# Half of one batch's first product as seven block products, sums moved, and a softmax divided later

## The chip, the core and the metric

The kernel runs on one core of a Trainium2 chip. Its engines each work through a queue of their own: TensorE (PE: matmuls; PEld: the loads of their stationary operand), VectorE (DVE), ScalarE (ACT), GpSimd (POOL), and SyncE (SP), which issues transfers. Matmul results land in PSUM, eight banks of 128 partitions x 512 fp32 each; everything else lies in SBUF. The metric is the device time of one execution in microseconds, 204.79 before the change (median of three runs).

## The reference

Per batch and head, tokens `x` (512 x 64) and a state (32 x 64) attend to one another; both results stand as rows of one matrix, which goes through a two-layer network.

```python
scores  = scale * x @ state.T;   a  = softmax(scores);   xread = a @ state     # 512 rows per head
scores2 = scale * state @ x.T;   a2 = softmax(scores2);  sread = a2 @ x        # 32 rows per head
...
x = attn_out.transpose(0, 2, 1, 3).reshape(B * S, H * D)    # B=8, 544 rows each, H*D=512
h = x @ w_in                                                # w_in 512 x 2048
g = np.maximum(0.01 * h, h)
return g @ w_out                                            # w_out 2048 x 512
```

Softmax here divides by the sum of the exponentials plus 1e-9. "Token softmax" is the one over tokens (`a2`).

## The kernel before

**First product.** For the 512 token rows of a batch the kernel does not form `xread`. Since `xread @ w_in = a @ (state @ w_in)`, it computes `M = state @ w_in` per head (`a_m`, psum tile `pm`), a matrix of 256 rows (8 heads x 32 states) and 2048 columns, held in SBUF as two groups of 128 rows, and then `a @ M` with `a` transposed (`aT`, two groups of 128 rows x 512 tokens). `ff1(a, hT, j)` does column block `j` of sixteen: two matmuls of 512 columns into a bank `ph` (line 372), then ACT's leaky relu into `hT[:, j]` (line 377). The tag `ph` has two banks.

**Second product.** From batch 2 on, `hT @ w_out` is done by `Fast` and `Batch`: the matrices are cut into 2 x 2 blocks and seven block products replace eight. Sums of blocks of `hT` (`su`, line 546) and of `w_out` (`tw`, line 523, made once in batch 2 by `weights_sum`) are operands. One *unit* is two matmuls of 256 columns (line 557); a block product has 8 units, numbered `n` in the order 1, 2, 6, 5, 7, 3, 4, and a batch 56. They use two banks (tag `py`, tile `yq`): some block products add onto what is in a bank, and in between the bank is copied out (`save`, line 566, ACT) or added to a saved one (`join`, line 569, DVE, or line 627, POOL).

**Order.** All queues but the transfers' details are written out by hand: `manual_schedule` keeps each engine's instructions in the order in which the program issues them. The loop over batches 2 to 7 has 16 steps `s`. Each step issues `ff1(s)` and then `PACE[s]` units (1 to 4) of the batch before, or, once those are used up, of its own (15 in all). So the units of batch 6 run between the column blocks of batch 7. Between them stand, at fixed steps, the attention of the next batch: scores, both softmaxes (`a_shift`, `a_exp`, `a_probs`; `a_max2`, `a_exp2`, `a_probs2`), `M`. After the loop a tail does the rest of batch 7's units, the first product of the 256 state rows (`FastIn`, also seven block products, whose operands are sums of `w_in`, tile `sw`, made by `w_sum` on DVE, and of `sread`, made by `x_sums`), and their second product.

**Token softmax.** `a_exp2` (ACT) writes the exponentials `e2` and their row sums `r2`. `a_probs2` (step 11 of the batch before, DVE) adds 1e-9, takes the reciprocal and multiplies both halves into `a2` (line 285). `a_a2t` transposes it with a transfer on SP's queue into `a2T` (step 0). At step 10 `a_sread_rows` forms `sread` in a bank of the tag `ph` (`psn`, line 318), and ACT copies it to `sr_n` (line 326). Behind it on PE, `a_m(nxt, 2, "ph")` needs two banks of that tag. Batch 7 differs: `a_sread` (step 8, line 300, tile `psr`) uses `a2T` as the stationary side's partner and writes `sr_t` directly (line 307).

**Places of the moved sums.** `weights_sum(0)` and `(2)` at step 3 of batch 2, `(1)` and `(3)` at step 8. `FastIn.w_sum(0)`, `(1)`, `(2)` at step 4 of batch 7, `(3)` and `x_sums` at step 10. At steps 0 to 3 DVE also makes the second halves of the `su` sums of the batch before, and at step 12 the first halves of its own.

Of the kernel before, what the change touches and what calls it, by code (L numbers as in the profile page):

```python
# [27 lines left out]
def kernel(  # L28
# [111 lines left out]
    st_t = [consts.tile([P, hi - lo, P], BF16, name=f"st_t{lo}") for lo, hi in groups]  # L140
    sr_t = consts.tile([P, B, NK, NS], BF16, name="sr_t")
    sr_n = {}

    stb0 = consts.tile([P, 4, D], BF16, name="stb0")

# [123 lines left out]

    def a_exp2(a, g):  # L270
        if g == 0:
            a.e2 = att.tile([P, 2, S], BF16, name="e2", tag="e2")
            a.r2 = att.tile([P, 2], FP32, name="r2", tag="r2")
        nc.scalar.activation(  # L274
            out=a.e2[:, g], in_=a.sc[:, g, :], func=AF.Exp,
            bias=a.m2s[:, g:g + 1], scale=SCALE, accum_out=a.r2[:, g:g + 1],
        )

    def a_probs2(a):
        nc.vector.tensor_scalar(out=a.r2[:], in0=a.r2[:], scalar1=1e-9, scalar2=None, op0=ALU.add)  # L280
        q2 = att.tile([P, 2], FP32, name="qc", tag="qc")
        nc.vector.reciprocal(q2[:], a.r2[:])
        a.a2 = att.tile([P, 2, S], BF16, name="a2", tag="a2")
        for g in range(2):
            nc.vector.tensor_scalar(
                out=a.a2[:, g, :], in0=a.e2[:, g, :],
                scalar1=q2[:, g:g + 1], scalar2=None, op0=ALU.mult,
            )

    def a_a2t(a):  # L290
        a.a2T = att.tile([P, 2, NT, P], BF16, name="a2T", tag="a2T")
# [19 lines left out]
    def a_sread_rows(some):  # L311

        ps = psum.tile([P, len(some), 2, D], FP32, name="psn", tag="ph")
        for u, a in enumerate(some):
            for g in range(2):
                for i in range(NT):
                    for k in range(NK):
                        nc.tensor.matmul(  # L318
                            ps[NS * k:NS * (k + 1), u, g, :],
                            lhsT=a.a2T[:, g, i, NS * k:NS * (k + 1)], rhs=a.xb[:, i, 2 * k + g, :],  # L320
                            start=(i == 0), stop=(i == NT - 1),
                        )
        c, b0 = divmod(some[0].b, 4)
        if c not in sr_n:
            sr_n[c] = consts.tile([P, 4, P], BF16, name=f"sr_n{c}", tag=("st0f", "stf2")[c])
        nc.scalar.copy(
            sr_n[c][:, b0:b0 + len(some)], ps[:].rearrange("p u g d -> p u (g d)")
        )

    def sread_t(c, n):  # L330
# [59 lines left out]
    class FastIn:  # L390
# [57 lines left out]
        def done(self, r, n, bank):  # L448
            R = self.R
            if n == 1:  # L450
                pool, tag, bufs = ((xpool, "xl", 1), (mpool, "M", 2))[r]
                self.sv[r] = pool.tile([P, 4, R * P], FP32, name=f"sf{r}", tag=tag, bufs=bufs)
            sv = {k: self.sv[r][:, i] for i, k in enumerate((1, 6, 5, 7))}
            flat = bank.rearrange("p q t -> p (q t)")

            def relu(i, c, src):
                nc.scalar.activation(
                    out=self.hT[:, 8 * i + R * r:8 * i + R * (r + 1), P * c:P * (c + 1)],
                    in_=src.rearrange("p (q t) -> p q t", q=R), func=AF.Prelu, alpha=0.01,
                )  # L460

            if n in (1, 6, 7):
                SCA(sv[n], flat)
            elif n == 5:
                VEC(sv[n], flat)
            if n in (2, 3):
                k = {2: 1, 3: 6}[n]
                nc.vector.tensor_tensor(out=sv[k], in0=flat, in1=sv[k], op=ALU.add)
                relu(0, n - 2, sv[k])
            elif n == 7:  # L470
                nc.gpsimd.tensor_tensor(out=sv[5], in0=sv[7], in1=sv[5], op=ALU.add)
            elif n == 4:
                relu(1, 1, sv[5])
                relu(1, 0, flat)

    class Y:
        pass
# [39 lines left out]
    def weights_sum(dst):  # L517
        u, v, op = (
            (B12, B11, ALU.subtract), (B11, tw[2], ALU.subtract),
            (B22, B12, ALU.add), (tw[1], B21, ALU.add),  # L520
        )[dst]
        with nc.allow_low_precision(reason="operands of a product"):
            nc.vector.tensor_tensor(out=tw[dst][:], in0=u[:], in1=v[:], op=op)
# [408 lines left out]
    for b in range(2, B):  # L932
        hT = hpool.tile([P, 16, S], BF16, name="hT", tag="hT")
        a = att_of[b]
        nxt = att_of[b + 1] if b + 1 < B else None
        now = Batch(b, hT)
        std = []
        if b == 2:
            std = [(i, 3) for i in range(2)] + [(i, jq) for i in range(2, NT) for jq in range(4)]

        def fill(s):
            n = (PACE2 if b == 2 else PACE)[s]
            left = min(n, len(before.units)) if before else 0
            if left:
                before.run(left)
            if n > left:
                now.run(n - left)

        for s in range(16):
            if s == 11:  # L950
                fill(s)
            ff1(a, hT, s)
            if s == 0:
                if b + 2 < B:
                    load_x(b + 2, nc.sync)
                    open_xb(b + 2)
                a_a2t(a)
                if before:
                    for n in (0, 1):
                        before.f.sums(n, 4, 8)  # L960
            elif s == 1:
                if nxt is not None:
                    a_scores(nxt)
                m_evict(a, 3, a_m(a, 3, "big"), SCA)
                if b == 2:
                    a_sread_rows([a0])
                if nxt is not None:
                    a_shift(nxt)
                if b + 2 < B:
                    for h in range(0, H, 2):  # L970
                        cast_x(b + 2, h, h + 2, POO)
                if before:
                    before.f.sums(2, 4, 8)
            elif s == 3:
                if before:
                    before.f.sums(3)
                if nxt is not None:
                    a_max2(nxt)
                if b == 2:
                    weights_sum(0)  # L980
                    weights_sum(2)
            elif s == 4:
                if b == 2:
                    state_t(1)
                elif b == 4:
                    sread_t(0, 4)
                elif b == 7:
                    sread_t(1, 3)
            elif s == 8:
                if nxt is None:  # L990
                    a_sread(a)
                if b == 2:
                    weights_sum(1)
                    weights_sum(3)
            elif s == 12:
                for n in range(3):
                    now.f.sums(n, 0, 4)
            if nxt is None:
                if s == 4:
                    fi = FastIn(None)  # L1000
                    for n in range(3):
                        fi.w_sum(n)
                elif s == 10:
                    fi.w_sum(3)
                    fi.x_sums()
            if s == (9 if b == 2 else 7) and b + 2 < B:
                a_open(att_of[b + 2], b + 2)
                a_xt_dma(att_of[b + 2])
            if nxt is not None:
                if s == 5:  # L1010
                    a_exp(nxt)
                elif s in (7, 8):
                    a_exp2(nxt, s - 7)
                    if s == 7:
                        a_probs(nxt)
                elif s == 11:
                    a_probs2(nxt)
                elif s in (12, 13):
                    SCA(nxt.M[:, s - 12, DM:2 * DM], pm1[:, s - 12, :])
            if std:  # L1020
                i, jq = std.pop(0)
                piece(1, h1, i, jq)
            elif s != 11:
                fill(s)
            if s == 10 and nxt is not None:
                a_sread_rows([a1, a2] if b == 2 else [a])
                pm0 = a_m(nxt, 0, "big")
                pm1 = a_m(nxt, 1, "sc")
                pm2 = a_m(nxt, 2, "ph")
                for g, copy in enumerate((VEC, SCA)):  # L1030
                    copy(nxt.M[:, g, 2 * DM:3 * DM], pm2[g][:])
                m_evict(nxt, 0, pm0, SCA)
        before = now
# [5 lines left out]
    for n in (0, 1):  # L1039
        before.f.sums(n, 4, 8)  # L1040
    fs = Fast(hs, P, [(att, "sh", 1), (att, "mrowb", 1), (att, "xT", 2), (att, "xT", 2)],
              {1: (att, "e1", 1), 6: (att, "qb", 1), 5: (att, "e2", 2), 7: (att, "e2", 2)})
    fi.hT = hs
    for n in (1, 2, 6, 5, 7, 3, 4):
        for r in range(2):
# [78 lines left out]
```

## Time and profile before

| | before |
|---|---|
| median of three runs | 204.79 us (204.59 to 205.09) |
| the profiled execution | 204.49 us |
| its span, first to last instruction | 202.7 us |
| granted TensorE clock, mean | 1.0 |
| steps 4 to 11 of batch 7 (162.73 to 173.20): busy PE, DVE, ACT, POOL | 10.47, 5.12, 5.54, 1.26 us of 10.47 |
| steps 0 to 3 of batch 7 (157.72 to 162.73): busy PE, DVE, ACT | 5.01, 4.80, 4.35 us of 5.01 |
| largest group, line 372 | 216 matmuls of 128x512, 62.3 us busy |
| line 285, the multiplications of the token softmax | 16, mean 350 ns |
| line 326, the copies of `sr_n` | 6, 265 to 372 ns |

An instruction's length in the profile is its start to its end; consecutive instructions of one engine can overlap, so the distance of two starts is often shorter than a length. A busy PE is therefore not a PE at its peak.

### The profile page before, as it was taken

How to read it: one execution, taken by the hardware profiler on the slowest of the kernel's cores; microseconds unless marked ns; L12 is line 12 of the kernel's file. 1: busy time of each engine (PE TensorE's matmuls, PEld its weight loads, DVE VectorE, ACT ScalarE, POOL GpSimd, SP SyncE). 2: the span in 40 equal slices, each digit the busy share in tenths (PEclk: the TensorE clock that was granted, in tenths of full speed). 3: DMA queues.
4: the chain of work that ended last, by engine and by line, in shares of the span. 5: the costliest groups of instructions: out<-in, count | busy, mean ns of one | idle time of the engine just before them, and what ended most of it. 6: DMA issues, size and time to landing. Idle time of an engine off the chain costs nothing.

```text
span 202.7 us, 4755 instructions
## 1 busy us (share of the span) xinstructions
PE 197.0 (97%) x1964; PEld 126.0 (62%) x1964; DVE 151.4 (75%) x230; ACT 143.7 (71%) x265; POOL 39.7 (20%) x66
## 2 busy tenths in 40 slices
PE   7899999999999999999999999999999999999993
PEld 2543544444344567766776767766767677799882
DVE  1677679599799969976996699769968853686612
ACT  3458848589869796978697878788778856467710
POOL 8831002021005005200251040200020002004250
PEclk9999999999999999999999999999999999999999
DMA  6999996999477895537946795250017100410035
GB/s 189 223 207 277 229 298 113 141 303 245 53 175 214 114 275 109 103 125 253 118 29 181 240 127 105 103 159 5 0 57 198 27 0 32 178 55 0 3 89 170
DMA packets 39733, 27.99 MB, mean 138 GB/s; under 512 B 25312, under 2 KB 36704, under 8 KB 39712
## 3 DMA queue, kind: packets, MB, share of 16 engines
q1 hardware_dynamic: 34512, 20.88, 44.6%
q0 software_dynamic: 4912, 6.55, 15.8%
q10 hardware_dynamic: 288, 0.26, 0.6%
q8 instruction: 15, 0.25, 0.5%
q14 instruction: 6, 0.05, 0.1%
HBM read 17.30 MB, written 8.91 MB: 129 GB/s over the span
## 4 chain that ended last, share of the span: by engine, by line
PE 96%; DVE 1%; ACT 1%; issue 0%
PE yq L557 36%; PE ph L372 23%; PE py L487 10%; PE pm L351 4%; PE pyw L487 3%; PE pf L441 3%; PE yu L557 3%; PE pspin L132 3%; PE ph L804 2%; PE sc L206 1%; PE psn L318 1%; PE phw L383 1%; PE php L804 1%; DVE M L365 1%; ACT xT L666 1%; PE scn L695 0%
## 5 line engine op out<-in xcount | busy, mean ns | idle before, releaser
L377 ACT ACTIVATE hT<-ph 128x512 bf16<-128x512 f32 x108 | 63.5, 604 | 22.0 <-PE ph L372 21.4
L372 PE MATMUL ph<-aT,M 128*128 128x512 bf16 x216 | 62.3, 379 | 0.0
L557 PEld LDWEIGHTS <-su 128*128 128x128 bf16 x416 | 39.7, 98 | 14.5 <-DVE su L546 1.7
L557 PEld LDWEIGHTS <-hT 128*128 128x128 bf16 x288 | 27.7, 98 | 11.7 <-issue 1.1
L557 PE MATMUL yq<-tw_xf,su 128*128 128x256 bf16 x192 | 27.2, 273 | 0.0
L105 POOL CAST xb<-xl 128x512 bf16<-128x512 f32 (+1 forms) x21 | 14.4, 724 | 65.2 <-PE ph L372 40.6
L557 PE MATMUL yq<-w_out_bf,hT 128*128 128x256 bf16 x192 | 27.0, 273 | 0.0
L372 PEld LDWEIGHTS <-M 128*128 128x128 bf16 x216 | 21.0, 98 | 9.3 <-issue 0.8
L546 DVE TENSOR_TENSOR su<-hT 128x1024 bf16<-128x1024 bf16 x24 | 16.8, 700 | 10.5 <-ACT hT L377 10.5
L487 PE MATMUL py<-w_out_bf,hT 128*128 128x512 bf16 x96 | 24.2, 379 | 0.0
L487 PEld LDWEIGHTS <-hT 128*128 128x128 bf16 x128 | 12.1, 98 | 14.6 <-issue 0.9
L627 POOL TENSOR_TENSOR yo<-sv,sv 128x512 f32<-128x512 f32 x6 | 7.8, 1300 | 54.1 <-ACT sv L566 42.7
L569 DVE TENSOR_TENSOR yo<-yq,sv 128x512 f32<-128x512 f32 x17 | 11.6, 685 | 6.5 <-PE yq L557 6.5
L566 ACT COPY sv<-yq 128x512 f32<-128x512 f32 x24 | 13.9, 585 | 2.0 <-PE yq L557 1.4
L365 ACT CAST M<-pm 128x1024 bf16<-128x1024 f32 x13 | 13.2, 1014 | 0.9 <-PE pm L351 0.8
L557 PE MATMUL yq<-w_out_bf,su 128*128 128x256 bf16 x96 | 13.1, 273 | 0.0
L557 PE MATMUL yq<-tw_x,su 128*128 128x256 bf16 x96 | 13.1, 272 | 0.0
L557 PE MATMUL yq<-tw_x,hT 128*128 128x256 bf16 x88 | 12.1, 273 | 0.0
L274 ACT ACTIVATE e<-sc,mcols 128x512 bf16<-128x512 f32 x16 | 11.1, 696 | 0.0
L216 DVE TRANSPOSE_TENSOR_REDUCE mrow<-sc 128x32 f32<-128x1024 f32 x7 | 8.7, 1245 | 2.4 <-PE sc L206 2.4
L266 DVE TENSOR_REDUCE mcol<-sc 128x2 f32<-128x1024 f32 x8 | 9.7, 1215 | 0.0
L247 DVE STREAM_TRANSPOSE qb<-qh 128x1024 bf16<-128x1024 bf16 x7 | 8.7, 1245 | 0.2
(147 smaller groups left out, 271.3 us busy)
## 6 DMA issues: line engine op xcount, KB each, us to landing
xl<-in_x_dram SPq DMA_DIRECT2D x5, 1024.0 KB, 7.1
out_dram<-yo SPq DMA_DIRECT2D x10, 512.0 KB, 3.0
w_in_bf<-in_moe_w_in_dram POOLq DMA_DIRECT2D x4, 512.0 KB, 9.1
w_out_bf<-in_moe_w_out_dram POOLq DMA_DIRECT2D x4, 512.0 KB, 17.0
out_dram<-ysb SPq DMA_DIRECT2D x8, 256.0 KB, 5.1
xf<-in_x_dram SPq DMA_DIRECT2D x2, 512.0 KB, 4.8
x<-in_x_dram POOLq DMA_DIRECT2D x2, 512.0 KB, 13.8
xl<-in_x_dram POOLq DMA_DIRECT2D x1, 1024.0 KB, 19.8
```

Source lines behind the costliest of these rows:

```text
L105: copy(xs[b][:, :, h0:h1].rearrange("p t h d -> p h t d"), xl[b][:, h0:h1].rearrange("p h (t d) -> p h t d", t=NT),)
L216: nc.vector.tensor_reduce(out=m1[:], in_=flat.rearrange("p (c j) -> p c j", j=NS), axis=AX.X, op=ALU.max, apply_transpose=True,)
L266: nc.vector.tensor_reduce(out=m2[:], in_=a.sc[:], axis=AX.X, op=ALU.max, negate=True)
L274: nc.scalar.activation(out=a.e2[:, g], in_=a.sc[:, g, :], func=AF.Exp, bias=a.m2s[:, g:g + 1], scale=SCALE, accum_out=a.r2[:, g:g + 1],)
L365: copy(a.M[:, :, cols], pm[:])
L372: nc.tensor.matmul(ph[:], lhsT=a.M[:, g, P * j:P * (j + 1)], rhs=a.aT[:, g, :], start=(g == 0), stop=(g == 1),)
L377: nc.scalar.activation(out=hT[:, j, :], in_=ph[:], func=AF.Prelu, alpha=0.01)
L487: nc.tensor.matmul(y.py, lhsT=hT[:, j, P * i:P * (i + 1)], rhs=w_out_bf[:, j, :], start=(j == 0), stop=(j == 15),)
L546: (eng or nc.vector).tensor_tensor(out=S[n][:, ms], in0=u[:, ms], in1=v[:, ms], op=op)
L557: nc.tensor.matmul(bank[:, i, :], lhsT=lhs[:, m, P * i:P * (i + 1)], rhs=rhs[:, m, :], start=(first and m == 0 and (i == 0 or of is not No ...
L566: copy(t[:], bank)
L569: nc.vector.tensor_tensor(out=dst, in0=bank, in1=self.sv[n][:], op=ALU.add)
```

## The change

1. **Half of batch 7's first product in seven block products.** Column blocks 0 to 3 and 8 to 11 go to a new class `FastLast`; blocks 4 to 7 are done at steps 0 to 3, 12 to 15 where they were. `FastLast` cuts `M` by rows (its two groups) and by columns (0 to 511 and 1024 to 1535), and `aT` by groups and by tokens (two times 256). It works in two rounds `r` of two 128-column blocks each; a product is two matmuls of 256 columns. At steps 4 to 11 products and units alternate. Operand sums are eight DVE instructions issued at step 1. Two banks of the tag `ph` hold a round; copies and additions in between are spread over ACT, DVE and POOL, and relus are put off (`late`) until the next copy.
2. **w_in's sums.** `w_sum(0)` moves to step 11 and `w_sum(2)` to step 12 of batch 6, `w_sum(1)` to step 6 and `w_sum(3)` to step 10 of batch 7; `x_sums` to step 13. `weights_sum(1)` and `(3)` move from step 8 to step 11 of batch 2.
3. **Token softmax.** In batches 0 to 6 the undivided exponentials are transposed and multiplied with `x`; the division is a multiplication with the reciprocals (`qall`) as `psn` is read out, on DVE instead of ACT. Batch 7 still divides first. `e2` has three buffers instead of two; `a2` loses its own.

```diff
     def a_probs2(a):
...
+        q2 = qall[:, a.b]
+        nc.vector.reciprocal(q2, a.r2[:])
+        a.a2 = a.e2
+        if a.b == B - 1:
+            a.a2 = att.tile([P, 2, S], BF16, name="a2", tag="e2", bufs=3)
...
     def a_sread_rows(some):
...
-        nc.scalar.copy(
-            sr_n[c][:, b0:b0 + len(some)], ps[:].rearrange("p u g d -> p u (g d)")
+        u0, n = some[0].b, len(some)
+        nc.vector.tensor_tensor(
+            out=sr_n[c][:, b0:b0 + n].rearrange("p u (g d) -> p u g d", g=2), in0=ps[:],
+            in1=qall[:, u0:u0 + n, :, None].to_broadcast([P, n, 2, D]), op=ALU.mult,
         )
...
+    class FastLast:
+        R, Q = 2, S // 2
+        ORDER = [(r, n) for r in range(2) for n in (1, 2, 6, 5, 7, 3, 4)]
...
+        def sums(self):
...
+                for n in (0, 2, 1, 3):
+                    S[n], T[n] = ws[:, n], xs[:, n]
...
+                        nc.vector.tensor_tensor(out=d, in0=u, in1=v, op=op)
...
+        def product(self):
+            r, n = self.todo.pop(0)
...
+            bank, sv = self.bank[2 if n in (2, 5, 3) else 1], self.sv
...
+            for q in range(R):
+                j = R * r + q
+                nc.tensor.matmul(
+                    bank[:, q, :], lhsT=lhs[:, P * j:P * (j + 1)], rhs=rhs,
+                    start=(n in (1, 2, 5) and q == 0), stop=True, skip_group_check=True,
+                )
...
+            if n in (1, 6, 7):
+                SCA(sv[n], flat)
+                self.flush()
+            elif n == 5:
+                VEC(sv[n], flat)
+            if n in (2, 3):
+                k = {2: 1, 3: 6}[n]
+                nc.vector.tensor_tensor(out=sv[k], in0=flat, in1=sv[k], op=ALU.add)
+                self.late.append((relu, 0, n - 2, sv[k]))
+            elif n == 7:
+                nc.gpsimd.tensor_tensor(out=sv[5], in0=sv[7], in1=sv[5], op=ALU.add)
+            elif n == 4:
+                relu(1, 0, flat)
+                self.flush()
+                self.late.append((relu, 1, 1, sv[5]))
...
         for s in range(16):
-            if s == 11:
+            fast = nxt is None and 4 <= s < 12
+            if fast:
+                n = 1 if s in (7, 11) else 2
+                k = PACE[s]
+                for i in range(n):
+                    fl.product()
+                    units((i + 1) * k // n - i * k // n)
+            elif s == 11:
                 fill(s)
-            ff1(a, hT, s)
+            if not fast:
+                ff1(a, hT, 4 + s if nxt is None and s < 4 else s)
```

More of the change, by code (lines that the diff above doesn't have):

```diff
@@ L142 @@
     sr_n = {}
+    qall = consts.tile([P, B, 2], FP32, name="qall")
     stb0 = consts.tile([P, 4, D], BF16, name="stb0")
@@ L271, in a_exp2 @@
         if g == 0:
-            a.e2 = att.tile([P, 2, S], BF16, name="e2", tag="e2")
+            a.e2 = att.tile([P, 2, S], BF16, name="e2", tag="e2", bufs=3)
             a.r2 = att.tile([P, 2], FP32, name="r2", tag="r2")
@@ L280, in a_probs2 @@
         nc.vector.tensor_scalar(out=a.r2[:], in0=a.r2[:], scalar1=1e-9, scalar2=None, op0=ALU.add)
[L281 to L288, printed above, removed]
+        q2 = qall[:, a.b]
[3 more added lines that the diff above has]
+            a.a2 = att.tile([P, 2, S], BF16, name="a2", tag="e2", bufs=3)
+            for g in range(2):
+                nc.vector.tensor_scalar(
+                    out=a.a2[:, g, :], in0=a.e2[:, g, :],
+                    scalar1=q2[:, g:g + 1], scalar2=None, op0=ALU.mult,
+                )
     def a_a2t(a):
@@ L474, in done, with __init__, relu, flush @@
                 relu(1, 0, flat)
+    class FastLast:
+        R, Q = 2, S // 2
+        ORDER = [(r, n) for r in range(2) for n in (1, 2, 6, 5, 7, 3, 4)]
+        def __init__(self, a, hT):
+            self.W = {(i, g): a.M[:, g - 1, P * 8 * (i - 1):P * (8 * (i - 1) + 4)] for i in (1, 2) for g in (1, 2)}
+            self.X = {(g, c): a.aT[:, g - 1, self.Q * (c - 1):self.Q * c] for g in (1, 2) for c in (1, 2)}
+            self.hT, self.S, self.T, self.sv = hT, {}, {}, {}
+            self.todo, self.late = list(self.ORDER), []
+        def sums(self):
+            W, X, S, T = self.W, self.X, self.S, self.T
+            ws = att.tile([P, 4, 4 * P], BF16, name="lw", tag="sh", bufs=1)
+            xs = att.tile([P, 4, self.Q], BF16, name="lx", tag="e1", bufs=1)
+            with nc.allow_low_precision(reason="operands of a product"):
+                for n in (0, 2, 1, 3):
+                    S[n], T[n] = ws[:, n], xs[:, n]
+                    for d, (u, v, op) in (
+                        (S[n], (
+                            (W[2, 1], W[2, 2], ALU.subtract), (S[0], W[1, 1], ALU.subtract),
+                            (W[2, 1], W[1, 1], ALU.subtract), (W[1, 2], S.get(1), ALU.add),
+                        )[n]),
+                        (T[n], (
+                            (X[1, 2], X[1, 1], ALU.subtract), (X[1, 1], T.get(2), ALU.subtract),
+                            (X[2, 2], X[1, 2], ALU.add), (T.get(1), X[2, 1], ALU.add),
+                        )[n]),
+                    ):
+                        nc.vector.tensor_tensor(out=d, in0=u, in1=v, op=op)
+        def product(self):
+            r, n = self.todo.pop(0)
+            R, Q = self.R, self.Q
+            if n == 1:
+                self.bank = {
+                    k: psum.tile([P, R, Q], FP32, name="pl", tag="ph")[:] for k in (1, 2)
+                }
+                homes = (("mrowb", 1), ("xT", 2)) if r == 0 else (("e2", 3), ("e2", 3), ("xT", 2))
+                ts = [
+                    att.tile([P, (2, 1)[t == "e2"], R * Q], FP32, name="ls", tag=t, bufs=c) for t, c in homes
+                ]
+                self.sv = dict(zip((1, 6, 5, 7), [t[:, i] for t in ts for i in range(t.shape[1])]))
+            bank, sv = self.bank[2 if n in (2, 5, 3) else 1], self.sv
+            lhs = {1: self.W[1, 1], 2: self.W[1, 2], 4: self.W[2, 2]}.get(n)
+            if lhs is None:
+                lhs = self.S[{3: 3, 5: 0, 6: 1, 7: 2}[n]]
+            rhs = {1: self.X[1, 1], 2: self.X[2, 1], 3: self.X[2, 2]}.get(n)
+            if rhs is None:
+                rhs = self.T[{4: 3, 5: 0, 6: 1, 7: 2}[n]]
+            for q in range(R):
[3 more added lines that the diff above has]
+                    start=(n in (1, 2, 5) and q == 0), stop=True, skip_group_check=True,
+                )
+            flat = bank.rearrange("p q t -> p (q t)")
+            def relu(i, c, src):
+                nc.scalar.activation(
+                    out=self.hT[:, 8 * i + R * r:8 * i + R * (r + 1), Q * c:Q * (c + 1)],
+                    in_=src.rearrange("p (q t) -> p q t", q=R), func=AF.Prelu, alpha=0.01,
+                )
+            if n in (1, 6, 7):
[13 more added lines that the diff above has]
+                self.late.append((relu, 1, 1, sv[5]))
+        def flush(self):
+            for f, *args in self.late:
+                f(*args)
+            self.late = []
@@ L941, in fill, with units @@
         def fill(s):
-            n = (PACE2 if b == 2 else PACE)[s]
+            units((PACE2 if b == 2 else PACE)[s])
+        def units(n):
             left = min(n, len(before.units)) if before else 0
@@ L991 @@
                     a_sread(a)
-                if b == 2:
-                    weights_sum(1)
-                    weights_sum(3)
             elif s == 12:
@@ L997 @@
                     now.f.sums(n, 0, 4)
+                if b == 6:
+                    fi.w_sum(2)
             if nxt is None:
[L999 to L1004, printed above, removed]
+                if s == 1:
+                    fl = FastLast(a, hT)
+                    fl.sums()
+                elif s in (6, 10):
+                    fi.w_sum({6: 1, 10: 3}[s])
+                elif s == 13:
+                    fl.flush()
                     fi.x_sums()
@@ L1017 @@
                     a_probs2(nxt)
+                    if b == 2:
+                        weights_sum(1)
+                        weights_sum(3)
+                    elif b == 6:
+                        fi = FastIn(None)
+                        fi.w_sum(0)
                 elif s in (12, 13):
@@ L1022 @@
                 piece(1, h1, i, jq)
-            elif s != 11:
+            elif s != 11 and not fast:
                 fill(s)
@@ L1041 @@
     fs = Fast(hs, P, [(att, "sh", 1), (att, "mrowb", 1), (att, "xT", 2), (att, "xT", 2)],
-              {1: (att, "e1", 1), 6: (att, "qb", 1), 5: (att, "e2", 2), 7: (att, "e2", 2)})
+              {1: (att, "e1", 1), 6: (att, "qb", 1), 5: (att, "e2", 3), 7: (att, "e2", 3)})
     fi.hT = hs
```

## The prediction

> **What bounds the kernel now.** I read the head of the page first, then its chain of waits, then the timelines of TensorE, VectorE and ScalarE through the last attention batch (batch 7, about 157.7 to 177.8 us), because that is where most of the edit lies.
>
> The page: busy times, and the chain that ended last.
>
> ```profile
> span 202.7 us, 4755 instructions
> PE 197.0 (97%) x1964; PEld 126.0 (62%) x1964; DVE 151.4 (75%) x230; ACT 143.7 (71%) x265; POOL 39.7 (20%) x66
> ...
> PE 96%; DVE 1%; ACT 1%; issue 0%
> ```
>
> PE is the chain for 96% of the span. Other engines matter only where PE stands still for them.
>
> The timeline of PE in the middle of batch 7 (start, length, engine, line, operands, count).
>
> ```profile
> 162.73 0.59 PE L372 MATMUL ph<-aT,M 128*128 128x512 bf16 x2
> 163.16 0.82 PE L557 MATMUL yq<-tw_xf,su 128*128 128x256 bf16 x6
> 163.82 0.59 PE L372 MATMUL ph<-aT,M 128*128 128x512 bf16 x2
> ```
>
> The starts fix the prices: two 512-column matmuls take 0.43 (163.16 - 162.73), so 0.216 each, and six of 256 columns 0.66, so 0.109 each. The stretch is dense: nothing here can be won but matmuls taken out.
>
> The timeline of VectorE (DVE) from the end of batch 6 on.
>
> ```profile
> 154.19 0.68 DVE L546 TENSOR_TENSOR su<-hT 128x1024 bf16<-128x1024 bf16 x1
> 154.91 0.69 DVE L546 TENSOR_TENSOR su<-su,hT 128x1024 bf16<-128x1024 bf16 x1
> 155.52 0.68 DVE L546 TENSOR_TENSOR su<-hT 128x1024 bf16<-128x1024 bf16 x1
> 157.90 0.69 DVE L546 TENSOR_TENSOR su<-hT 128x1024 bf16<-128x1024 bf16 x1 [1.69 <-ACT hT L377]
> 158.62 0.69 DVE L546 TENSOR_TENSOR su<-su,hT 128x1024 bf16<-128x1024 bf16 x1
> 159.23 0.68 DVE L569 TENSOR_TENSOR yo<-yq,sv 128x512 f32<-128x512 f32 x1
> 159.83 0.68 DVE L546 TENSOR_TENSOR su<-hT 128x1024 bf16<-128x1024 bf16 x1
> 160.43 1.22 DVE L546 TENSOR_TENSOR su<-hT,su 128x2048 bf16<-128x2048 bf16 x1
> 161.56 1.22 DVE L411 TENSOR_TENSOR sw<-w_in_bf 128x2048 bf16<-128x2048 bf16 x1
> ```
>
> DVE idles 1.69 us before 157.90 and then runs without a break. Its instructions follow one another 0.60 apart though each is 0.68 long (1.13 apart for 1.22); where one reads the result of the one before it, 0.72.
>
> The timeline of VectorE and ScalarE (ACT) in the tail, for the smaller forms.
>
> ```profile
> 188.08 0.42 DVE L546 TENSOR_TENSOR su<-su,hs 128x512 bf16<-128x512 bf16 x1
> 188.43 0.42 DVE L546 TENSOR_TENSOR su<-hs 128x512 bf16<-128x512 bf16 x1
> ```
> ```profile
> 188.50 0.62 ACT L457 ACTIVATE hs<-sf 128x512 bf16<-128x512 f32 x1
> 189.02 0.58 ACT L457 ACTIVATE hs<-pf 128x512 bf16<-128x512 f32 x1
> 189.49 1.07 ACT L566 COPY sv<-yq 128x512 f32<-128x512 f32 x2
> ```
>
> A 128x512 bf16 sum takes 0.35 in a row. ACT takes 0.52 from SBUF, 0.48 from PSUM, in a row; a waiter sees the whole 0.62 or 0.58.
>
> **The change, part by part. Matmuls.** Eight of the sixteen column blocks of batch 7's first product lose 16 matmuls of 512 columns (16 x 0.216 = 3.46) and get 14 block products of two 256-column matmuls each (28 x 0.109 = 3.05): -0.41 us. This is the whole gain on the path.
>
> **The sums of the block product, on DVE.** In step 1 of batch 7 stand four 128x512 bf16 sums (4 x 0.35) and four 128x256 ones; two of the latter (the sums of L423) fill 0.49 us with 0.29 long each, so 0.20 apart: 4 x 0.20. Together 2.2 us, in front of the whole-length sum that now starts at 160.43. Besides, two of w_in's four sums now stand in steps 11 and 12 of batch 6: from 154.19 on, 1.13, then 0.72 + 0.61 + 0.60 for the three half sums, then 1.13, so the queue comes free at 158.38, not at the 157.90 at which ACT lets it go on: 0.48 late; the idle 1.69 hid the rest. Then 0.72 + 0.61 + 0.60 + 0.60 as before brings 160.91, the eight sums 163.13, the whole-length sum (1.14) 164.27. The three w_in sums that stood behind it are gone, but the first thing behind it is now the join of block products 1 and 2, which reads PSUM: 0.69 (L569's form) gives 164.96, and 0.05 to wake PE (early in the kernel ACT's 0.58 copy of 8.16 lets PE start at 8.80) gives 165.01.
>
> PE wants that bank for block product 5. From 162.73: product 1, one unit of the second product, product 2, two units, product 6, two units, each 0.218, is eight of them: 164.47. **First stall: 0.54 us.** All units behind it on PE's queue wait with it.
>
> **Saves and relus.** ACT gets, for 8 relus, 6 saves and 8 relus; DVE 2 saves and 4 joins; POOL two additions (1.27, L471), of which the first would run from 166.8 to 168.1, just ahead of POOL's own addition for batch 6, which came at 168.26: 0. After the first half's last product ends at 167.19 (165.01 + 2.18), ACT has in one row from 167.39: relu out of PSUM, relu out of SBUF, a save of the second product, the save of block product 1, a relu, the two sr_t copies (0.25 each, L307), the save of product 6: 0.48 + 0.52 + 0.48 + 0.48 + 0.52 + 0.50, then 0.58 seen whole: 170.95, and 0.05. PE is ready for product 7 at 170.92 (with psr's 0.46 in between, 167.95 to 168.41 before): stall 0.08. With the lengths 0.60 in place of the distances it is 0.3. Product 3 wants DVE's save of product 5, queued behind batch 6's join: that starts at 170.46, 0.62, then 0.69: 171.77 and 0.05, against 171.65: stall 0.17. **Together 0.25.** Two more waits have margins of 0.05 (product 6 on the save of 1, the first product 4 on the save of 7): 0.05 for the pair.
>
> **Softmax division.** DVE loses two multiplications (0.61 together) in seven batches. Only the transposes on SP's queue waited for them; these keep their place behind the load of x and the output writes, may go earlier, and are read only at the next step 10 (issue at 154.35, in batch 7 read by psr at 167.95), so 0. ACT loses the copies sr_n (0.27), DVE gets a multiplication out of PSUM of 128x128, which no row shows: between 0.18 (128x16, L711) and 0.42 (128x256, L569), 0.29 by the line through both. PE waits for that bank when the third pm product starts, 151.58; the copy starts at 151.19. Up to 0.34 it is hidden, and DVE was idle there from 150.5 to 151.96. If it isn't, 0.1 in each of five batches. In batch 2 it has 256 columns: 0.42 against 0.37, and PE already waits there: +0.05. weights_sum's two sums move 2 steps later, out of its way; they put the half sums of batch 2 off to 73.9, whose first reader comes at 75.25: 0. The last two w_in sums lie in DVE time that was idle (5.25 us before 170.43); the four x sums follow the last join of batch 6 (until about 174.7) and three half sums (2.0) and take 1.0, so they end at about 177.7, before ACT lets DVE go on in the tail (177.94 + 0.48): 0.
>
> **Sum.** -0.41 + 0.54 + 0.25 + 0.05 + 0.05 = +0.48: span 203.2 for 202.7. The profiled execution took 204.49, 0.30 under the median of 204.79; I put the difference on the median: **205.3 us**.
>
> **A rule that speaks against it.** The Trainium skill, "VectorE: DVE Perf Modes", section Terms, says that every DVE operation is followed by a pipeline flush and that the next cannot issue until the pipe is empty. The starts 0.60 apart at lengths of 0.68 don't agree with it as it stands; taken to the letter it gives the first rival below its time.
>
> **Rivals.**
> - *Whole lengths on DVE* (slower). If instructions of these forms cost their length, the queue is free at 154.27 + 1.22 + 2.05 + 1.22 = 158.76, + 2.73 = 161.49, + 4 x 0.42 + 4 x 0.285 = 164.31, + 1.22 + 0.69 + 0.05 = 166.27: first stall 1.8; with the later ones at whole lengths, 0.6: -0.41 + 2.4 = +2.0, 206.8. It decides from the join's start: each 0.1 after 163.73 is 0.1 on the span. Against it: the distances above. For it: operands of M and aT in slices, that no row shows.
> - *The bank behind psn* (slower). The multiplication takes over 0.34, or stands behind another one: 0.1 in each of five batches, 0.1 to 0.2 in batch 2: +0.48 + 0.6 = 205.9. For it: only 0.04 of margin. Against: DVE is idle there.
> - *The join in time* (not slower). If the eight sums take 0.2 us each, or PE comes 0.5 later, the first stall falls away and the rest shrinks to 0.2: -0.41 + 0.2 = 204.6, at best, without any stall, 204.4. For it: PE has units of the second product between all block products. Against: DVE has no idle time left there.
>
> **Chances.** A measurement of this kernel tells about 0.3% (0.61 us) from no change: below 204.18 is faster, above 205.40 slower. The forecast 0.55, with its own range 204.9 to 205.8, which the bound cuts (0.30 same, 0.25 slower). Whole lengths 0.12, slower. The bank 0.15 (0.11 slower, 0.04 same). In time 0.18: 204.4 is still inside 0.3%, so 0.11 same, 0.07 faster for what I overlook. In sum 0.07 faster, 0.45 same, 0.48 slower. Range 204.4 to 206.5: the low end is the gain without stalls, the high end reaches most of the way to whole lengths.
>
> **What would show it.** In the profile after: 28 block-product matmuls about 0.109 apart; a hole of some 0.5 us in PE before product 5 of the first half, released by DVE's join, whose start is near 164.3; small holes in the second half, released by ACT and DVE saves; batches 3 to 6 as long as before (21.05 us each), and the tail from the last first-product matmul on unchanged. No hole before product 5, or a hole over 1 us, proves the DVE sum wrong; a longer batch 3 proves the price of the multiplication wrong.

## The result, and the profile after

| | before | after |
|---|---|---|
| median of 17 runs each | 204.73 us | 205.09 us |
| ratio, after over before | | 1.0023, 95% interval 1.0014 to 1.0031 |
| span of the profiled execution | 202.7 us | 203.0 us |
| PE's scores (L206, now L207) at about 40 us | 40.18 | 40.00 |
| from there to batch 6's scores | 97.67 us | 97.86 us |
| of these, scores to scores, batches 2, 3, 4, 5 | 21.07, 21.05, 21.06, 21.05 us | 21.12, 21.08, 21.14, 21.08 us |
| from batch 6's scores to the tail's first product (L441, now L446) | 39.92 us | 40.24 us |
| from that product to the end | 24.95 us | 24.95 us |

The kernel became slower by 0.23%, 0.47 us by the ratio. The rows below the span cut it at starts of PE instructions, as the timeline has them. The time to the first cut differs from one execution to the next by more than the change (39.96 to 40.74 us over all profiles of this study); in 13 of the 14 profiles the chain has a transfer there, of x, of the state or of w_in, and in the first profile of the kernel before it has none. What sets that time isn't shown. From that cut to the end two profiles of the kernel before took 162.53 and 162.55 us, two of the changed one 163.05 and 163.08, so +0.52 us in the profile. Batches 3 to 5 repeat to 0.01 us wherever their code is the same. Batch 2 doesn't: with the code of the changed kernel it took 21.12 to 21.28 us in five profiles, so a difference of up to 0.16 there says nothing about an edit to batch 7.

The page of the changed kernel, head and chain:

```profile
span 203.0 us, 4789 instructions
PE 196.8 (97%) x1976; PEld 126.8 (62%) x1976; DVE 155.1 (76%) x236; ACT 145.4 (72%) x265; POOL 44.4 (22%) x68
...
PE 90%; DMA 5%; POOL 2%; DVE 1%; issue 0%; POOLq 0%
```

PE has 12 matmuls more (28 for 16) and 0.2 us less of busy time, in a span 0.3 longer. The DMA in the chain is a transfer of w_in, from 4.67 to 15.08 us, that landed last in this execution.

PE's timeline around the first hole (L534 is a block product, L648 a unit):

```profile
163.87 0.38 PE L534 MATMUL pl<-lx,lw 128*128 128x256 bf16 x2
164.09 0.38 PE L648 MATMUL yq<-tw_xf,su 128*128 128x256 bf16 x2
164.31 0.38 PE L648 MATMUL yq<-tw_x,su 128*128 128x256 bf16 x2
164.98 0.38 PE L534 MATMUL pl<-lx,lw 128*128 128x256 bf16 x2 [0.29 <-DVE ls L553]
```

Starts lie 0.22 apart up to 164.31; the next is 0.67 later. So PE stands still for 0.45 us before product 5 of the first round, and the profile names DVE's join (L553) as the releaser; the 0.29 in brackets is less than the hole, since the last matmul, 0.27 long where the next usually starts after 0.11, counts as busy to its end.

VectorE's timeline ahead of that join:

```profile
157.30 1.22 DVE L416 TENSOR_TENSOR sw<-w_in_bf 128x2048 bf16<-128x2048 bf16 x1
...
160.96 0.42 DVE L511 TENSOR_TENSOR lw<-M 128x512 bf16<-128x512 bf16 x1
161.29 0.28 DVE L511 TENSOR_TENSOR lx<-aT 128x256 bf16<-128x256 bf16 x1
...
163.11 1.22 DVE L637 TENSOR_TENSOR su<-hT,su 128x2048 bf16<-128x2048 bf16 x1
164.24 0.68 DVE L553 TENSOR_TENSOR ls<-pl,ls 128x512 f32<-128x512 f32 x1
```

No row here has an idle bracket, nor has one of those left out: the join's inputs are there from about 163.8 (ACT's save of product 1 runs from 163.19 to 163.77), but it starts at 164.24, when the queue lets it. The second and third hole, 0.13 before product 7 and 0.11 before product 3 of the second round, are the gaps before the two L534 here:

```profile
170.46 0.60 PE L648 MATMUL yq<-tw_x,hT 128*128 128x256 bf16 x4
171.03 0.38 PE L534 MATMUL pl<-lx,lw 128*128 128x256 bf16 x2
171.25 0.60 PE L648 MATMUL yq<-tw_x,hT 128*128 128x256 bf16 x4
171.79 0.38 PE L534 MATMUL pl<-aT,lw 128*128 128x256 bf16 x2
```

Four 256-column matmuls end their turn 0.44 after they begin; 171.03 - 170.46 is 0.57, 171.79 - 171.25 is 0.54 (0.13 and 0.11 by the unrounded starts). What each waits for is the save of the product before it in its bank, ACT's of product 6 and DVE's of product 5:

```profile
170.39 0.59 ACT L547 COPY ls<-pl 128x512 f32<-128x512 f32 x1
```
```profile
171.05 0.68 DVE L550 COPY ls<-pl 128x512 f32<-128x512 f32 x1
```

They end at 170.98 and 171.73, and PE starts 0.05 and 0.06 later.

The rest is at the bank behind psn, in batches 2 to 6. Its release, and the loads with which PE goes on into that bank, in batch 6 before and then after:

```profile
151.19 0.27 ACT L326 CAST sr_n<-psn 128x128 bf16<-128x128 f32 x1 [0.67 <-PE psn L318]
151.50 0.10 PEld L351 LDWEIGHTS <-st_t 64*32 64x32 bf16 x6
```
```profile
151.20 0.29 DVE L330 TENSOR_TENSOR sr_n<-psn,qall 128x128 bf16<-128x128 f32 x1 [0.67 <-PE psn L321]
151.55 0.10 PEld L356 LDWEIGHTS <-st_t 64*32 64x32 bf16 x6 [0.17 <-issue]
```

In both kernels PE goes on 0.05 after the release ends (0.051 and 0.055 by the unrounded times). So it waited for the release before the change too, and what the release takes longer (0.29 us for 0.27) goes through to PE. Batches 3 and 5 show the same. In batch 4 of the changed kernel the multiplication also starts later, 0.55 us after psn's first matmul for 0.50 in the others; with that, the 24 pm matmuls behind psn take 0.96 us there for 0.87. The row doesn't say what it waits for ("issue"):

```profile
109.04 0.29 DVE L330 TENSOR_TENSOR sr_n<-psn,qall 128x128 bf16<-128x128 f32 x1 [0.73 <-issue]
```

### The profile page after: what moved, and what is told of

Same layout as the page of the kernel before. It is cut to its first block, busy times and chain, and to the rows that moved or that the text cites. A ratio compares the mean times of both kernels' runs of the same rounds, so it can differ in the third digit from the quotient of the medians.

```text
span 203.0 us, 4789 instructions
## 1 busy us (share of the span) xinstructions
PE 196.8 (97%) x1976; PEld 126.8 (62%) x1976; DVE 155.1 (76%) x236; ACT 145.4 (72%) x265; POOL 44.4 (22%) x68
## 4 chain that ended last, share of the span: by engine, by line
PE 90%; DMA 5%; POOL 2%; DVE 1%; issue 0%; POOLq 0%
PE yq L648 36%; PE ph L377 21%; PE py L578 10%; DMA w_in_bf<-in_moe_w_in_dram 5%; PE pm L356 4%; PE pyw L578 3%; PE pf L446 3%; PE yu L648 3%; PE ph L895 2%; PE pl L534 2%; PE sc L207 1%; PE psn L321 1%; PE phw L388 1%; POOL w_in_bf L118 1%; DVE M L370 1%; PE pxt L945 0%
## 5 line engine op out<-in xcount | busy, mean ns | idle before, releaser
L382 ACT ACTIVATE hT<-ph 128x512 bf16<-128x512 f32 x100 | 58.9, 605 | 16.3 <-PE ph L377 15.8
L377 PE MATMUL ph<-aT,M 128*128 128x512 bf16 x200 | 57.7, 379 | 0.0
L648 PEld LDWEIGHTS <-su 128*128 128x128 bf16 x416 | 39.7, 98 | 13.5 <-DVE su L637 1.9
L648 PEld LDWEIGHTS <-hT 128*128 128x128 bf16 x288 | 27.7, 98 | 11.5 <-issue 1.1
L105 POOL CAST xb<-xl 128x512 bf16<-128x512 f32 (+1 forms) x21 | 15.4, 772 | 61.7 <-DMA xl<-in_x_dram 48.9
L648 PE MATMUL yq<-tw_xf,su 128*128 128x256 bf16 x192 | 27.4, 273 | 0.0
L648 PE MATMUL yq<-w_out_bf,hT 128*128 128x256 bf16 x192 | 27.0, 273 | 0.0
L377 PEld LDWEIGHTS <-M 128*128 128x128 bf16 x200 | 19.4, 98 | 8.9 <-issue 0.8
L648 PE MATMUL yq<-tw_x,su 128*128 128x256 bf16 x96 | 13.4, 273 | 0.0
L648 PE MATMUL yq<-w_out_bf,su 128*128 128x256 bf16 x96 | 13.3, 273 | 0.0
L648 PE MATMUL yq<-tw_x,hT 128*128 128x256 bf16 x88 | 12.4, 273 | 0.0
L225 DVE STREAM_TRANSPOSE mrowb<-mrow 128x1024 f32<-128x1024 f32 x7 | 8.7, 1245 | 0.2
```

The source lines that it names most:

```text
L105: copy(xs[b][:, :, h0:h1].rearrange("p t h d -> p h t d"), xl[b][:, h0:h1].rearrange("p h (t d) -> p h t d", t=NT),)
L377: nc.tensor.matmul(ph[:], lhsT=a.M[:, g, P * j:P * (j + 1)], rhs=a.aT[:, g, :], start=(g == 0), stop=(g == 1),)
L382: nc.scalar.activation(out=hT[:, j, :], in_=ph[:], func=AF.Prelu, alpha=0.01)
L648: nc.tensor.matmul(bank[:, i, :], lhsT=lhs[:, m, P * i:P * (i + 1)], rhs=rhs[:, m, :], start=(first and m == 0 and (i == 0 or of is not No ...
```

## The experiments

Two theories stand against each other throughout: that the difference is made of DVE's late join, two smaller waits and the bank behind psn; or that one of these places is innocent and the time comes from elsewhere (the block product as such, the start, the rest of the edit). Each run was timed in several rounds beside the kernel before on the same chip; "from 40 us" is the stretch from PE's scores at about 40 us to the end, in the profile.

**late_sums**: three operand sums out of the row in front of the join.

```diff
-                for n in (0, 2, 1, 3):
...
+            self.some(("S", 0), ("T", 0), ("T", 2), ("S", 1), ("T", 1))
...
             elif n == 5:
                 VEC(sv[n], flat)
+                if r == 0:
+                    self.some(("T", 3))
...
+                if (r, n) == (0, 2):
+                    self.some(("S", 2), ("S", 3))
```

`some` issues the named sums: five at step 1, one behind the save of product 5, two behind the join of products 1 and 2.

> The changed kernel with three of the eight operand sums of the block product taken out of the row at step 1: the sums of product 7 (column blocks, S2) and product 3 (S3) are issued behind the join of products 1 and 2, and the token sum of product 4 (T3) behind the save of product 5. Theory (VectorE's queue is late for that join): 0.33 + 0.33 + 0.20 = 0.87 us go from in front of the join, its start moves from 164.24 to where product 2 and the save of 1 let it, about 163.8, and the hole of 0.46 us before product 5 is gone; product 3 may wait 0.1 more. 0.3 to 0.5 us under the changed kernel, ratio to the kernel before 0.9995 to 1.001. Rival (the hole is the time that ScalarE's copy and the join take after product 2, wherever the queue stands): the hole stays, ratio 1.002.

Ratio 1.0012 (1.0002 to 1.0023), from 40 us 162.75. PE and DVE:

```profile
165.02 0.38 PE L654 MATMUL yq<-tw_x,su 128*128 128x256 bf16 x2
165.27 0.38 PE L536 MATMUL pl<-lx,lw 128*128 128x256 bf16 x2
```
```profile
164.53 0.69 DVE L557 TENSOR_TENSOR ls<-pl,ls 128x512 f32<-128x512 f32 x1 [0.35 <-ACT ls L549]
```

The join now waits for ACT's save, and 0.03 us of the 0.46 is left. The rival falls: where DVE's queue stood was the cause. The ratio's midpoint lies a little above what was expected, its interval covers it; the stretch went from 163.05 to 162.75: 0.43 less in batch 7, 0.14 more in batch 2, which the edit doesn't touch (PE waited longer there for the bank behind psn).

**soft_alone**: the softmax part, put alone into the kernel before (`qall`, undivided `e2`, the multiplication out of PSUM on DVE; `weights_sum(1)` and `(3)` stay at step 8).

> The kernel before with the softmax part of the change alone. Theory (the only price is the bank behind psn, released by VectorE instead of ScalarE): batches 3 to 6 longer by 0.02 to 0.08 us each, as in the changed kernel; in batch 2 the multiplication stands behind the two sums of w_out at step 8, which end at 68.36, and reads 256 columns, so the bank comes free at about 68.8 instead of 68.1 and PE waits 0.6 longer. In all +0.6 to +0.9 us, ratio 1.003 to 1.0045. Rival (the division out of the way frees VectorE and is worth something or nothing): ratio 0.998 to 1.001.

Ratio 1.0081 (1.0063 to 1.0098), from 40 us 164.48, +1.95, over twice the expected loss. Batches 3 to 5 are longer by 0.03, 0.08 and 0.03, as in the changed kernel. The rest is one hole in batch 2; DVE, then PE:

```profile
68.81 1.23 DVE L528 TENSOR_TENSOR tw_x<-tw_xf,w_out_bf 128x2048 bf16<-128x2048 bf16 x1
69.96 0.42 DVE L330 TENSOR_TENSOR sr_n<-psn,qall 128x256 bf16<-128x256 f32 x1
```
```profile
70.43 0.41 PE L356 MATMUL pm<-w_in_bf,st_t 64*32 64x512 bf16 x7 [1.43 <-DVE sr_n L330]
```

The place is the expected one, the size is not: the two sums of w_out start 1.2 us later against PE than before, because DVE's multiplication at step 1 of batch 2 stands ahead of the row maxima and waits for PE there, and because two other sums then fall together with POOL's casts and take 1.56 and 1.62 us for 1.22. In the changed kernel, where the sums of w_out stand behind the multiplication, batch 2 takes 21.12 us for 22.84 here; that move is what the softmax part needs.

**soft_off**: the changed kernel with the softmax part undone.

> The changed kernel with the softmax part undone. Theory: what is left is batch 7, -0.41 of matmuls and 0.69 of holes, +0.28 us on the kernel before, ratio 1.001 to 1.002; batches 2 to 6 as long as before. Rival (batch 7 costs nothing and all is the softmax or the start): ratio 1.000. Rival (the softmax part helps batch 7): above 1.0025.

Ratio 1.003 (1.0015 to 1.0045), from 40 us 162.91: +0.38, of which batch 7 has +0.30 and batch 2 0.07; batches 3 to 5 take 21.06, 21.05 and 21.05 us as before. So batch 7 costs about 0.3 by itself, and the lengthening of batches 3 to 5 belongs to the softmax part. The ratio's midpoint lies above the expected range, even in that of the second rival, but its interval reaches into the range, and by the trace the softmax part doesn't help batch 7 (+0.30 without it, +0.32 with it). By the ratio this run isn't better than the changed kernel; the intervals overlap widely.

**w1_early**: one sum of w_in more in front of the join.

```diff
                 if b == 6:
                     fi.w_sum(2)
+                    fi.w_sum(1)
...
-                elif s in (6, 10):
-                    fi.w_sum({6: 1, 10: 3}[s])
+                elif s == 10:
+                    fi.w_sum(3)
```

> The changed kernel with one more of w_in's sums put in front: w_sum(1) at step 12 of batch 6, behind w_sum(2), instead of at step 6 of batch 7. Theory (VectorE's queue has no idle time left ahead of the join): 1.13 us more in front go to the hole before product 5 in full, 0.46 to 1.6 us, and its absence at 167.4 gives nothing back: 0.9 to 1.2 us above the changed kernel, ratio to the kernel before 1.0065 to 1.008. Rival (join bound by ScalarE and PE): no change, 1.002.

Ratio 1.0091 (1.0072 to 1.011), from 40 us 164.24: 1.19 over the changed kernel, for 1.13 us of work. PE:

```profile
161.48 1.05 PE L648 MATMUL yq<-tw_xf,su 128*128 128x256 bf16 x8 [0.49 <-DVE su L637]
...
166.56 0.38 PE L534 MATMUL pl<-lx,lw 128*128 128x256 bf16 x2 [0.98 <-DVE ls L553]
```

The added time comes back in full in batch 7 (1.13; the other 0.05 lies in batch 2), but in two holes, not in the one that was expected: 0.45 earlier, where the units of the second product's block product 6 now wait for the second half of their sums, and 1.15 before product 5 in place of 0.46. The ratio's midpoint is above the expected 1.008, the interval covers it.

**w_old**: w_in's sums back at step 4 (three) and step 10 of batch 7.

> The changed kernel with w_in's sums back where they stood: three at step 4 of batch 7, the fourth at step 10. Theory (VectorE's queue): the join of products 1 and 2 is in time, since 0.48 us are gone in front of it, but the three sums (1.13 + 1.25 + 1.13) now stand between it and the save of product 5, which product 3 waits for: a hole of about 2.9 us moves from before product 5 to before product 3. +2.8 to +3.3 us on the kernel before, ratio 1.0135 to 1.016. Rival (VectorE is busy for half of this stretch only, so three sums fit in): ratio at most 1.003.

Ratio 1.0189 (1.0156 to 1.0222, four runs), from 40 us 165.60: +3.07 on the kernel before, of which batch 7 has 2.71 and batch 2 0.21.

```profile
169.47 0.38 PE L534 MATMUL pl<-aT,lw 128*128 128x256 bf16 x2 [2.66 <-DVE ls L550]
```

The hole before product 5 is down to 0.03 and one of 2.82 stands before product 3, as the queue's order says. DVE's mean load tells nothing here. The ratio is above the expected range and above the stretch's 1.015; the four runs spread over 1.5 us, and the two longest (209.07 and 209.18) show a granted clock of 0.99.

**late_soft_off**, run twice: `late_sums` and `soft_off` together.

> The changed kernel with the softmax part undone and with the three operand sums of the block product issued later. Theory: both prices found so far are gone, batches 3 to 6 as before, batch 7 at -0.41 + 0.03 + 0.13 + 0.11 = -0.14 us; ratio 0.999 to 1.0. Rival (something else in the edit costs 0.2 us or more): above 1.001.

> late_soft_off once more, beside the kernel before on one chip. Theory: from 40 us to the end 162.4 us, 0.1 less than before, ratio 0.999 to 1.001. Rival (a cost outside the stretch): ratio over 1.001 again with the start longer.

Ratios 1.0011 (0.9997 to 1.0025) and 1.0001 (0.9988 to 1.0014), from 40 us 162.42 and 162.41: 0.11 and 0.12 under the kernel before, 39.79 for 39.92 in batch 7. The first ratio lies above the range and by its midpoint with the rival, the second doesn't; neither interval excludes 1. What the block product can win without the first hole and the softmax part is seen in the trace and not in the time.

**late_soft_off_sread**: the same with psr and its copies at step 11.

```diff
-            elif s == 8:
-                if nxt is None:
-                    a_sread(a)
...
+                elif s == 11:
+                    a_sread(a)
```

> As the one before, with the state read of batch 7 (psr and its two copies on ScalarE) moved from step 8 to step 11. Theory (the hole before product 7 of the second round is ScalarE's row of copies, with 0.5 us of sr_t in it): that hole of 0.13 goes; the one before product 3 stays; batch 7 at -0.27 us, ratio 0.9985 to 0.9995. Rival (the row of relus is long enough without sr_t): as the one before.

Ratio 1.0048 (1.0033 to 1.0063), from 40 us 163.25. The hole before product 7 went, but the one before product 3 grew from 0.10 to 0.16 and three came: 0.37 and 0.08 before products 6 and 5, and 0.35 in the units at 175.6. Neither the theory nor its rival foresaw that.

```profile
169.47 0.38 PE L531 MATMUL pl<-lx,lw 128*128 128x256 bf16 x2 [0.20 <-ACT ls L544]
```

psr's 0.46 us of PE at step 8 were the cover of ACT's save of product 1; and the last sum of w_in, whose buffer was psr's operand `xb`, now waited for psr (1.23 us, to 174.07), with DVE's join of batch 6 behind it, which the units at 175.6 wait for.

**best**: the same with DVE's join of batch 6's products 5 and 3 put behind the save of product 5.

> As the one before, with VectorE's join of batch 6's block products 5 and 3 issued behind the save of product 5 of the second round instead of in front of it. Theory: the last hole (0.11, before product 3 of the second round) goes too; batch 7 at -0.38 us, no hole over 0.05 in steps 4 to 11, ratio 0.998 to 0.999. Rival (the block products have a hole of their own, from one bank used five times in a row): holes of 0.1 or more stay.

Ratio 1.003 (1.0015 to 1.0044), from 40 us 162.99. The hole before product 3 went, so it was that join; those of the moved psr stayed (0.36, 0.07 and 0.35), so the time missed its range. Holes of over 0.1 staying was the rival's sign, but these came with psr and are gone again in the next run, where one bank is used as often. The fourth sum of w_in shows the buffer:

```profile
174.04 1.23 DVE L411 TENSOR_TENSOR sw<-w_in_bf,sw 128x2048 bf16<-128x2048 bf16 x1 [1.23 <-PE psr L300]
```

**holes_shut**: `late_soft_off` with psr at step 8, its two copies behind the save of product 6, and the join behind the save of product 5.

```diff
                 SCA(sv[n], flat)
                 self.flush()
+                if (r, n) == (1, 6):
+                    a_sread_copies(a)
...
             elif n == 5:
                 VEC(sv[n], flat)
+                if r == 0:
+                    self.some(("T", 3))
+                else:
+                    before.end()
```

`before.end()` is the join of batch 6.

> late_soft_off with psr left at step 8, where it covers the save of product 1, but its two copies on ScalarE issued behind the save of product 6, and with VectorE's join of batch 6's products 5 and 3 behind the save of product 5. Theory: the holes of 0.13 and 0.10 go, steps 4 to 11 of batch 7 have no hole over 0.05; batch 7 at -0.37 us, from 40 us to the end 162.2 us, ratio 0.998 to 0.9995. Rival (each cover taken opens another hole, as with psr moved): 162.4 or more.

Ratio 0.9998 (0.9988 to 1.0007), from 40 us 162.50. The holes between block products are gone but for 0.04. A new one of 0.2 stands in the units at 175.1, which write into a bank that DVE's other join of batch 6 empties; that join stands behind the last sum of w_in, 1.93 us long here, which began while a POOL addition ran (172.13 to 173.40):

```profile
172.55 1.93 DVE L414 TENSOR_TENSOR sw<-w_in_bf,sw 128x2048 bf16<-128x2048 bf16 x1
174.41 0.68 DVE L668 TENSOR_TENSOR yo<-yq,sv 128x512 f32<-128x512 f32 x1
```

So the rival was right: shutting the holes made a new one, and batch 7 comes to -0.16 for an expected -0.37. Of the 162.50, 0.10 over the kernel before is in batch 2, which these moves don't touch. In time it cannot be told from the kernel before.

**before_again, after_again**: both kernels once more, on one chip.

> The kernel before against itself, on the chip of the next three: ratio 1.0 within its interval, and a profile whose time up to the second batch's scores (40.2 us in the first profile) says how far the start alone moves from one execution to the next. All theories expect the stretch from there to the end at 162.5 us.

> The changed kernel once more. Theory: from the scores at 40 us to the end 163.0 us (+0.5), ratio 1.0015 to 1.0035, whatever its start does. Rival (the start carries the difference): the stretch as before, the ratio with the start.

Ratios 1.0005 (0.9996 to 1.0013) and 1.0019 (1.0006 to 1.0032), from 40 us 162.55 and 163.08. Their starts were 40.36 and 39.96: the start does not carry the difference.

## Why the prediction was right

*The matmuls.* -0.41 was the price of 28 for 16; the whole balance of steps 4 to 11 confirms it: 10.75 us (162.78 to 173.53) for 10.47, which is +0.28, and -0.41 + 0.46 + 0.13 + 0.11 is +0.29.

*The first hole.* Forecast 0.54 with the join at 164.27; it came at 164.24, and the hole was 0.46, as PE itself arrived at 164.53 instead of 164.47. late_sums took it away by making the queue in front of the join shorter, w1_early made it 1.15 by making it longer. With that the rivals of whole lengths (a hole of 1.8) and of a join in time (no hole) fall.

*The two later holes.* Forecast 0.08 and 0.17, measured 0.13 and 0.11. The second belongs to the join of batch 6 in front of a save, as said (best shut it). Of the first it isn't shown which of ACT's instructions matter: holes_shut shut it by putting the copies of sr_t later, with the join moved at the same time.

*The pair with margins of 0.05.* Priced at 0.05, cost nothing.

*The softmax part.* Batch 2 was priced at 0.05 and the stretch up to batch 3's scores grew by 0.05. Batches 3 to 6 were priced at 0, because PE was taken to need the bank at 151.58, so that the multiplication's 0.29 (measured 0.29) would be hidden. This step was wrong: PE goes on into that bank at 151.50, 0.05 after the copy's end, so it already waited for the copy and there was no margin to spend. They cost 0.03, 0.08, 0.03 and about 0.03, 0.17 in all: the 0.025 by which the multiplication is longer, in each, and its later start in batch 4. By the prediction's own sign, a longer batch 3, the price was wrong; the rival of this bank was right in the mechanism and had 0.1 per batch. soft_off showed that it is this part. That the moved sums of w_out cost nothing was right within what batch 2 varies by (21.08 in late_soft_off for 21.07); that without the move it would cost 1.8 us was not seen ahead (soft_alone).

*The rule on VectorE.* The row of eight sums starts at 160.96, 161.29, 161.50: 0.33 after one of 0.42, 0.21 after one of 0.28. The Trainium skill, "VectorE: DVE Perf Modes", section Terms, would have the next wait for an empty pipe. Read by the recorded lengths, as the first rival did, the first hole would have been 1.8, and it was 0.46, so lengths are not what a queue is stepped by here. Whether the recorded end is the moment at which the pipe is empty, no run here shows.

*The sum.* +0.48 forecast, +0.52 in the profile, 0.47 by the ratio: the hole 0.08 smaller, the softmax 0.17 larger, the pair 0.05 smaller. The mechanism in batch 7 was forecast hole by hole; that the total came within 0.04 is partly luck, since the errors have opposite signs.

## What to carry to other kernels

Where one engine is dense, a saving of its work is paid out only if each release it waits for is in time; step the releasing engines' queues by the distances between starts, not by lengths or by mean loads, and look for what stands in front of the releasing instruction, even work of another stage. Work that seems to stand in the way (psr) can be the cover of another wait, and a sum that is moved takes its buffer's last reader with it: each such move wants its own look at who reads, who waits and what was hidden. When the whole saving is 0.4 us, a wait that is to be hidden has to be read at the instruction that waits: the bank behind psn was priced at nothing by a time 0.08 too late, while the trace had PE starting 0.05 after the release all along.

## What the hardware showed beyond what was expected

A bf16 sum of 128x2048 on VectorE took 1.20 to 1.23 us alone and 1.56 to 1.93 when it began while POOL was at work, as here in the changed kernel:

```profile
166.71 1.26 POOL L556 TENSOR_TENSOR ls<-ls 128x512 f32<-128x512 f32 x1 [17.32 <-ACT ls L547]
```
```profile
167.38 1.67 DVE L416 TENSOR_TENSOR sw<-sw,w_in_bf 128x2048 bf16<-128x2048 bf16 x1
```

The sum ends 1.08 us after POOL's addition (167.97). So it is in all 14 traces: 46 of these sums began with 0.4 us or more of a POOL instruction still to run, and each ended 1.07 or 1.08 us after that instruction. So the sum isn't slowed in proportion, it ends about as if it began its work when POOL was done. The joins of the block products, which read one operand from PSUM, kept their 0.69 us beside the same additions. The Trainium skill, "GPSIMD Engine Reference", section 1. Specifications, says that POOL's SBUF interfaces are shared with VectorE and that VectorE instructions with two SBUF inputs contend; these rows agree. The changed kernel gives POOL two more additions in batch 7, and both lengthened a sum there that PE didn't wait for (1.67 and 1.58 us); in holes_shut PE did wait for the join behind such a sum.
